# First preparation of a fused attention and expert kernel: remaining keys behind the first head, weight words behind the keys

## The chip, the cores and the metric

The kernel runs on one core of a Trainium2 chip. The metric is the device time of one execution in microseconds. Before the change three executions took 706.53, 705.54 and 706.43 us, a median of 706.43 us.

## The reference

Attention over 2 batches, 8 heads, 576 positions and a head size of 64, with a threshold: scores further than tau below a row's maximum are set aside before the softmax. Its output, 1152 tokens of 512, goes through a max of three linear layers and an output layer, and then through four experts of 1024 hidden units, weighted by normalised shares. All of it is asked for in float32; tau is 0.02, and the first layers' weights arrive as float64.

```python
scores = scale * q @ k.T
thresh = scores.max(-1, keepdims=True) - tau
scores = where(scores >= thresh, scores, -1e9)
attn = exp(scores - scores.max(-1, keepdims=True)); attn /= attn.sum(-1, keepdims=True) + 1e-9
x = (attn @ v).transpose(0, 2, 1, 3).reshape(1152, 512)
x = maximum(maximum(x @ w1, x @ w2), x @ w3) @ w_out
p = probs / (probs.sum(-1, keepdims=True) + 1e-9)
out = sum(p[:, e:e+1] * (maximum(x @ m_w1[e], 0) @ m_w2[e]) for e in range(4))
```

## The kernel before, in words

Every float32 product is made of three float32r products: each operand is cut into a high part (a rounded copy, made by ScalarE) and a low part (the rest, made by VectorE or GpSimd).

The program has three regions. **Region A** is the attention of batch 0 (`attention_fast`, L583): four jobs of two heads each, 9 steps to a job, 36 steps. A step makes one tile of scores, 128 query rows by 576 keys: `qk` (L382, four matmuls on TensorE), `peak` (L407, the row maximum, VectorE), `power` (L417, the exponential, ScalarE), `weigh` (L421, threshold and row sum, VectorE), `norm` (L427, GpSimd), `turn` (L437, transposes on TensorE), `cut_hi` and `cut_lo` (L477, L491), and per group of steps `gather` (L516, the product with the values). In this region the order of instructions on each engine is chosen by the framework's scheduler from a simulated timeline, except where `tc.issue_after(x)` puts an instruction behind x on x's engine. **Region B** holds the layers on batch 0's tokens and, woven in, the attention of batch 1; there the order on TensorE, VectorE, ScalarE and GpSimd is the order in the program. **Region C** is the rest of batch 1's tokens. The queue of SyncE (SP), which issues most DMAs, is ordered by the scheduler throughout.

Job 0 has a preparation of its own, `prep_first` (L283). `load_first` (L185) loads head 0's keys, the remaining 64 keys of both heads (`krem`, L193) and head 1's keys on SP, and the same of the queries (`qnat`, `qrem`) on ScalarE's queue. 512 of the 576 keys of a head are the main part. `head(h)` (L296) cuts a head's queries (`split`, L291: L292 copies keys, L293 the high part, L294 the low part), transposes keys (L300) and queries (L302), and writes the high keys (L305), the queries (L306) and the low keys (L307). The remaining keys go through L312 and L313 (transposes), L317 and L318. `qk` of step 0 needs all of head 0 and the remaining keys. Before any data is there, `spin` (L197) runs 14 matmuls on a constant tile; more follow behind the scores of steps 1, 2 and 3, 22, 8 and 8 of them (`SPINS_A`).

The layers' work follows a plan in columns of matmul work: `plan.at(when, fn)` files a function, and `stream.flush(when)` calls all that are due. A float64 weight block goes through the stages of `block` (L759): `words` (L775, load 512 KB as 32-bit words on SP), `exponent` (L791, ScalarE), `clamp` (L801, GpSimd), `low3` (L798), `merge` (L804) and `sign` (L809) on VectorE, `keep` (L813, stores the float32 block to DRAM for region C on SP: L818 for the first layers, L821 for the output layer), `hi` (L765, ScalarE) and `lo` (L769, GpSimd). The first three blocks are due before region A's steps: `stream.flush(-55000)` calls two `words`, `stream.flush(-READY)` the third and the stages of all three. `load_probs` and `norm_probs` (L1262, L1270) load and normalise the experts' shares. `sums_ahead` (L964) loads kept blocks on ScalarE's queue, adds quarters of them on GpSimd (L962) and stores the sums (L982).

Of the kernel before, what the change touches and what calls it, by code (L numbers as in the profile page):

```python
# [22 lines left out]
def fused_kernel(ctx: ExitStack, tc: tile.TileContext, q, k, v, tau, w1, w2, w3, w_out, probs, m_w1, m_w2, out):  # L23
# [46 lines left out]
    SPINS, SPINS_A = 14, (22, 8, 8)  # L70
# [114 lines left out]
    def load_first(job):  # L185

        for nm, src, eng in (("k", k, nc.sync), ("q", q, nc.scalar)):
            n = 2 if nm == "k" else 1
            t = atile([P, 2, NC, n, D], F32, "KN" if n == 2 else "qnat")
            r = atile([P, n, D], F32, f"{nm}rem")  # L190
            main = src[job.b, 2 * job.p:2 * job.p + 2, 0:MAIN, :].rearrange("h (p c) d -> p h c d", c=NC)
            eng.dma_start(out=t[:, 0, :, 0, :], in_=main[:, 0])
            eng.dma_start(out=r[:, 0, :], in_=src[job.b, 2 * job.p:2 * job.p + 2, MAIN:S, :])  # L193
            eng.dma_start(out=t[:, 1, :, 0, :], in_=main[:, 1])
            job.raw[nm] = (t, r)
# [86 lines left out]

    def prep_first(job):  # L283
# [12 lines left out]
        def head(h):  # L296
            split(QN[:, h * NC:(h + 1) * NC], qt[:, h, :, 0, :], kt[:, h])
            tk, tq = ptile_at("U", [P, MAIN]), ptile_at("U", [P, MAIN])
            for c in range(NC):
                nc.tensor.transpose(tk[:, c * P:(c + 1) * P], flat(kt[:, h, c]), ident)  # L300
            for c in range(NC):
                nc.tensor.transpose(tq[:, c * P:(c + 1) * P], flat(QN[:, h * NC + c]), ident)  # L302
            ko, qo = (0, W + REM)[h], (0, W + 2 * REM)[h]
            d1 = K1[:, ko:ko + MAIN]
            nc.scalar.activation(out=d1, in_=tk, func=AF.Copy)  # L305
            nc.scalar.activation(out=QS[:, qo:qo + MAIN], in_=tq, func=AF.Copy, scale=qscale)  # L306
            nc.vector.tensor_tensor(out=K2[:, ko:ko + MAIN], in0=tk, in1=f32(d1), op=ALU.subtract)  # L307

        head(0)
        split(QN[:, 2 * NC:], qr, kr[:, None])  # L310
# [6 lines left out]
        nc.scalar.activation(out=k1r, in_=trk, func=AF.Copy)  # L317
        nc.vector.tensor_tensor(out=k2r, in0=trk, in1=f32(k1r), op=ALU.subtract)  # L318
        yield
        head(1)  # L320
# [100 lines left out]
    def weigh(st):  # L421

        sv, _, ev = views(st)
        nc.vector.scalar_tensor_tensor(  # L424
            out=ev, in0=sv, scalar=st.stat["thr"], in1=ev, op0=ALU.is_ge, op1=ALU.mult, accum_out=st.stat["sum"])
# [157 lines left out]
    def attention_fast(jobs, modes):  # L583
# [5 lines left out]
        load_first(jobs[0])  # L589
        stream.flush(-55000)  # L590
        load_job(jobs[0], "v")
# [3 lines left out]
        for _ in start:  # L595
            pass
        stream.flush(-READY)
        back.add(values(jobs[0]))
# [10 lines left out]
        for i in range(n + 3):  # L609
# [34 lines left out]
            if nxt:  # L644
                at["raised"] = power(st)
                if i == n - NEARLY:
                    at["nearly"] = at["raised"]
# [5 lines left out]
            if nxt:  # L653
                weigh(st)
                if i:
                    turn(steps[i - 1])
            if st and not nxt:
# [101 lines left out]
    def block(use, shape, tag, bufs, load, lags, name=None, g=0, src=None, apart=False):  # L759
# [15 lines left out]
        def words():  # L775
            b["words"] = mo["words"].tile(shape + [2], U32, tag="words", name="words", bufs=NW)
            with ExitStack() as held:
                if "fourth" in at:
                    held.enter_context(tc.issue_after(at["fourth"].ins))
                nc.sync.dma_start(out=b["words"], in_=src)  # L780
# [32 lines left out]
        def keep():  # L813
# [5 lines left out]
            else:  # L819
                kept[name] = dp.tile(shape, F32, name=f"kept_{name}")  # L820
                nc.sync.dma_start(out=kept[name], in_=b["raw"])  # L821
# [262 lines left out]
    def max_mixed():  # L1084
# [31 lines left out]
        for f in range(0, NF, 2):  # L1116
            for w in range(3):
                ahead = f == 0 or w > 0
                for c in range(2 if ahead else 0):
                    sums_ahead(MAX0 + 6000 + AHEAD * k, (f"w{w}_{f // 2}", c), lambda w=w, f=f, c=c: kept[f"w{w}_{f // 2}"][:, c::2])  # L1120
# [3 lines left out]
        for f in range(0, NF2 // 2, 2):  # L1124
            for c in range(2):
                rows = m_w1[0].rearrange("(j c p) f -> c p j f", j=2, p=P)[c]
                sums_ahead(MAX0 + 6000 + AHEAD * k, (f"e{f}", c), lambda f=f, rows=rows: rows[:, :, f * P:(f + 2) * P].rearrange("p j (i f) -> p j i f", i=2))
# [164 lines left out]
    plan.at(MAX0 - 60000, norm_probs)  # L1292
# [101 lines left out]
```

## Time and profile before

| | |
|---|---|
| three executions | 706.53, 705.54, 706.43 us; median 706.43 |
| the profiled execution: its own time, its span | 707.25 us, 705.4 us |
| busy, share of the span | TensorE 98%, VectorE 67%, ScalarE 52%, GpSimd 70% |
| DMA | 95.17 MB, mean 135 GB/s |

The span runs from the first to the last instruction of the program; the execution's own time is 1.85 us longer. TensorE is busy in nearly all of it, so the places where it is idle, and the stretches in which it does work that serves nothing but its clock, are few and can be counted one by one. The page prints the granted clock in tenths of full speed.

### The profile page before, as it was taken

Reading aid. Unit: us, or ns where it says so; the run is one execution under the profiler, and the core shown is the slowest. Engines: PE = TensorE matmul, PEld = TensorE weight load, DVE = VectorE, ACT = ScalarE, POOL = GpSimd, SP = SyncE. Lnnn points to the kernel's source line nnn. Section 1 sums busy time; section 2 is a strip of 40 time slices with the busy share of each in tenths; the row PEclk is TensorE's granted clock in tenths of the full one; section 3 lists DMA queues with packets and bytes.
Section 4 is the critical chain, followed back from the end, with each engine's and each line's share of the span. In section 5 each row is a group of like instructions: output and inputs, shape, how many; then the busy total and the mean of one; then the engine's idle time right before and its main releaser. Section 6 shows DMA issues by size and latency. Waiting matters only on the chain.

```text
span 705.4 us, 11938 instructions
## 1 busy us (share of the span) xinstructions
PE 692.7 (98%) x3975; PEld 614.7 (87%) x3975; DVE 470.6 (67%) x1056; ACT 365.7 (52%) x774; POOL 493.4 (70%) x567
## 2 busy tenths in 40 slices
PE   7999999999999999999999999999999999999997
PEld 7988888877778888888888889999998998998996
DVE  5998898875467767677676567874644644653653
ACT  5989875544455555474545344446533433433430
POOL 4879876876585657576586477778569669669660
PEclk9999999999999999999999999999999999999999
DMA  6764506977888458365433643453122222322103
GB/s 185 181 140 97 150 1 201 276 228 224 229 225 218 118 140 231 109 174 152 120 120 89 213 158 123 150 165 122 58 90 90 77 74 90 91 66 88 56 1 75
DMA packets 108808, 95.17 MB, mean 135 GB/s; under 512 B 27340, under 2 KB 91852, under 8 KB 108748
## 3 DMA queue, kind: packets, MB, share of 16 engines
q1 hardware_dynamic: 91498, 83.24, 41.4%
q10 hardware_dynamic: 17218, 11.18, 5.4%
q8 instruction: 32, 0.52, 0.3%
q14 instruction: 28, 0.23, 0.1%
q0 software_dynamic: 32, 0.00, 0.0%
HBM read 69.09 MB, written 13.37 MB: 117 GB/s over the span
## 4 chain that ended last, share of the span: by engine, by line
PE 77%; POOL 7%; ACT 4%; DVE 4%; issue 4%; DMA 3%; SPq 0%; POOLq 0%; DVEq 0%; ACTq 0%
PE ps L1245 64%; PE u L534 5%; PE s L401 4%; PE t L441 3%; POOL a L769 3%; DMA raw<-in_moe_w_dram 1%; ACT em L419 1%; POOL hl L875 1%; POOL b L801 1%; DMA K<-KN 1%; ACT a L765 1%; POOL em L431 1%; DVE raw L809 1%; DMA krem<-in_k_dram 1%; DVE em L424 1%
## 5 line engine op out<-in xcount | busy, mean ns | idle before, releaser
L1245 PE MATMUL ps<-b,hh 128*128 128x512 f32 (+1 forms) x584 | 185.0, 391 | 0.0
L769 POOL TENSOR_TENSOR b<-raw,b 128x512 fp32r<-128x512 f32 x64 | 82.9, 1301 | 67.8 <-ACT b L765 67.7
L1245 PEld LDWEIGHTS ps<-b,hh 128*128 128x128 f32 x584 | 108.4, 188 | 20.8
L1245 PE MATMUL ps<-b,hl 128*128 128x512 f32 (+1 forms) x292 | 114.1, 391 | 0.0
L769 POOL TENSOR_TENSOR a<-raw,a 128x512 fp32r<-128x512 f32 (+1 forms) x58 | 72.8, 1257 | 35.8 <-ACT a L765 33.6
L1209 DVE SCALAR_TENSOR_TENSOR acc<-ps,pr,acc 128x512 f32<-128x512 f32 (+1 forms) x64 | 47.4, 741 | 73.2 <-PE ps L1245 72.9
L431 POOL TENSOR_SCALAR em<-em,st_r,one 128x576 f32<-128x576 f32 x70 | 58.0, 830 | 43.7 <-DVE st_r L430 35.7
L419 ACT ACTIVATE em<-s,st_negm 128x576 f32<-128x576 f32 x72 | 53.6, 744 | 60.4 <-DVE st_negm L412 53.1
L1245 PE MATMUL ps<-y0h,a 128*128 128x512 f32 x256 | 83.7, 400 | 0.3 <-POOL a L769 0.3
L412 DVE TENSOR_REDUCE st_negm<-s 128x1 f32<-128x576 f32 x72 | 54.2, 754 | 33.6 <-PE s L401 32.6
L1245 PE MATMUL ps<-bt,sh 128*128 128x320 f32 x300 | 69.9, 309 | 0.0
L424 DVE SCALAR_TENSOR_TENSOR em<-s,st_thr,em 128x576 f32<-128x576 f32 x72 | 58.6, 814 | 12.1 <-ACT em L419 10.8
L1030 POOL TENSOR_TENSOR sl<-s,sh 128x512 fp32r<-128x512 f32 x50 | 64.6, 1313 | 0.0
L1245 PEld LDWEIGHTS ps<-b,hl 128*128 128x128 f32 x292 | 54.9, 188 | 10.3
L765 ACT ACTIVATE a<-raw 128x512 fp32r<-128x512 f32 (+1 forms) x66 | 39.5, 603 | 36.7 <-DVE raw L809 14.2
L1017 POOL TENSOR_TENSOR dl<-wraw,dh 128x512 fp32r<-128x512 f32 (+1 forms) x50 | 50.1, 1023 | 8.3 <-ACT dh L1012 8.3
L1136 ACT ACTIVATE hh<-ps 128x320 fp32r<-128x320 f32 x64 | 27.4, 439 | 54.5 <-DVE ps L1063 54.5
L1245 PEld LDWEIGHTS ps<-y0h,a 128*128 128x128 f32 x256 | 47.2, 189 | 9.4 <-POOL a L769 0.8
L1245 PE MATMUL ps<-y0l,a 128*128 128x512 f32 x128 | 51.4, 401 | 0.0
L1245 PEld LDWEIGHTS ps<-bt,sh 128*128 128x128 f32 x300 | 51.1, 188 | 0.0
L401 PE MATMUL s<-K,QS 128*128 128x288 f32 x264 | 49.3, 309 | 1.4 <-DVE em L424 0.7
L1245 PE MATMUL ps<-x0h,a 128*128 128x512 f32 (+1 forms) x168 | 46.4, 363 | 0.7 <-POOL a L769 0.7
(227 smaller groups left out, 1723.5 us busy)
## 6 DMA issues: line engine op xcount, KB each, us to landing
raw<-in_moe_w_dram SPq DMA_DIRECT2D x96, 256.0 KB, 2.8
words<-in_moe_w_dram SPq DMA_DIRECT2D x18, 512.0 KB, 4.0
wraw<-in_moe_w_dram SPq DMA_DIRECT2D x16, 512.0 KB, 3.4
kept_w<-raw SPq DMA_DIRECT2D x18, 256.0 KB, 3.0
wraw<-kept_w SPq DMA_DIRECT2D x9, 512.0 KB, 3.6
K<-KN SPq DMA_DIRECT2D x14, 288.0 KB, 5.3
K<-KN SPq DMA_DIRECT2D x14, 256.0 KB, 4.1
sraw<-kept_w ACTq DMA_DIRECT2D x14, 256.0 KB, 3.9
```

Source lines behind the costliest of these rows:

```text
L401: st.whole = nc.tensor.matmul(st.s[:, kh, 0:HS], lhsT=l, rhs=r, start=i == 0, stop=i == len(terms) - 1)
L412: nc.vector.tensor_reduce(out=st.stat["negm"], in_=views(st)[0], op=ALU.max, axis=AX.XY, negate=True)
L419: return nc.scalar.activation(out=ev, in_=sv, func=AF.Exp, bias=st.stat["negm"])
L424: nc.vector.scalar_tensor_tensor(out=ev, in0=sv, scalar=st.stat["thr"], in1=ev, op0=ALU.is_ge, op1=ALU.mult, accum_out=st.stat["sum"])
L431: last = (nc.vector if swift else nc.gpsimd).tensor_scalar(out=em, in0=em, scalar1=re, scalar2=one, op0=ALU.mult, op1=ALU.mult)
L534: at["valued"] = nc.tensor.matmul(pv, lhsT=l, rhs=r, start=i == 0, stop=i == len(terms) - 1)
L765: nc.scalar.activation(out=b["hi"], in_=b["raw"], func=AF.Copy)
L769: nc.gpsimd.tensor_tensor(out=b["lo"], in0=b["raw"], in1=f32(b["hi"]), op=ALU.subtract)
L1017: nc.gpsimd.tensor_tensor(out=rows(b["dl"], x), in0=src, in1=f32(rows(b["dh"], x)), op=ALU.subtract)
L1030: nc.gpsimd.tensor_tensor(out=rows(b["sl"], slice(x, x + 2)), in0=rows(b["s"], slice(x, x + 2)), in1=f32(rows(b["sh"], slice(x, x + 2))), ...
L1209: nc.vector.scalar_tensor_tensor(out=accs[t][:, cols], in0=ps, scalar=pe, in1=accs[t][:, cols], op0=ALU.mult, op1=ALU.add)
L1245: nc.tensor.matmul(banks[x], lhsT=l, rhs=r, start=i == 0, stop=i == count - 1)
```

## The change

- `load_first` remembers the loads of the remaining keys and queries. The first `words` load gets a dependency on both: it is issued when they have landed.
- The values of job 0 are loaded ahead of the `words`.
- The split of the remaining queries and keys is issued behind head 0's last instructions on ScalarE and VectorE (`behind`). Head 1's query transposes, copies and low keys are issued behind the remaining keys' copies and behind step 0's scores.
- The third `words`, the stages of the three blocks and the values' cut are called after step 0's `weigh` and issued behind step 0's `power` on ScalarE and `weigh` on VectorE.
- The spins behind step 1's scores go from 22 to 14.
- `norm_probs` goes from 60000 columns ahead of `MAX0` to 24000 behind it (`MAX0` is where the plan's output layer ends).
- The output layer's kept blocks are stored from ScalarE's queue and no longer from SP.
- `sums_ahead` goes 22000 columns later.

```diff
-    SPINS, SPINS_A = 14, (22, 8, 8)
+    SPINS, SPINS_A = 14, (14, 8, 8)
...
-            eng.dma_start(out=r[:, 0, :], in_=src[job.b, 2 * job.p:2 * job.p + 2, MAIN:S, :])
+            at["rest", nm] = eng.dma_start(out=r[:, 0, :], in_=src[job.b, 2 * job.p:2 * job.p + 2, MAIN:S, :])
...
+    def behind(*steps):
+        held = ExitStack()
+        for x in steps:
+            held.enter_context(tc.issue_after(x.ins))
+        return held
...
-        def head(h):
+        def head(h, *held):
             split(QN[:, h * NC:(h + 1) * NC], qt[:, h, :, 0, :], kt[:, h])
...
-            nc.vector.tensor_tensor(out=K2[:, ko:ko + MAIN], in0=tk, in1=f32(d1), op=ALU.subtract)
-
-        head(0)
-        split(QN[:, 2 * NC:], qr, kr[:, None])
+            with behind(*held):
+                for c in range(NC):
+                    nc.tensor.transpose(tq[:, c * P:(c + 1) * P], flat(QN[:, h * NC + c]), ident)
+                nc.scalar.activation(out=d1, in_=tk, func=AF.Copy)
+                stacked = nc.scalar.activation(out=QS[:, qo:qo + MAIN], in_=tq, func=AF.Copy, scale=qscale)
+                return stacked, nc.vector.tensor_tensor(out=K2[:, ko:ko + MAIN], in0=tk, in1=f32(d1), op=ALU.subtract)
+
+        with behind(*head(0)):
+            split(QN[:, 2 * NC:], qr, kr[:, None])
...
-        nc.scalar.activation(out=k1r, in_=trk, func=AF.Copy)
-        nc.vector.tensor_tensor(out=k2r, in0=trk, in1=f32(k1r), op=ALU.subtract)
+        high = nc.scalar.activation(out=k1r, in_=trk, func=AF.Copy)
+        low = nc.vector.tensor_tensor(out=k2r, in0=trk, in1=f32(k1r), op=ALU.subtract)
         yield
-        head(1)
+        head(1, high, low, (yield))
...
+        load_job(jobs[0], "v")
         stream.flush(-55000)
-        load_job(jobs[0], "v")
         start = prep_first(jobs[0])
         next(start)
         qk(steps[0])
-        for _ in start:
+        next(start)
+        try:
+            start.send(steps[0].whole)
+        except StopIteration:
             pass
-        stream.flush(-READY)
-        back.add(values(jobs[0]))
...
-                weigh(st)
+                weighed = weigh(st)
                 if i:
                     turn(steps[i - 1])
+                else:
+                    with behind(raised, weighed):
+                        stream.flush(-READY)
+                        back.add(values(jobs[0]))
+                        back.advance(2)
...
-                nc.sync.dma_start(out=b["words"], in_=src)
+                load = nc.sync.dma_start(out=b["words"], in_=src)
+            for nm in "" if kept.setdefault("words", 0) else "kq":
+                tc.add_manual_dep(load.ins, at["rest", nm].ins.name, ...)
+            kept["words"] = 1
...
-                nc.sync.dma_start(out=kept[name], in_=b["raw"])
+                nc.scalar.dma_start(out=kept[name], in_=b["raw"])
...
-                    sums_ahead(MAX0 + 6000 + AHEAD * k, ...
+                    sums_ahead(MAX0 + 28000 + AHEAD * k, ...
...
-    plan.at(MAX0 - 60000, norm_probs)
+    plan.at(MAX0 + 24000, norm_probs)
```

## Rows read from the trace of the kernel before

**Rows 1.** Waits of TensorE over the span: us in total, times, longest us.
```profile
PE t L312 <- DVE krem L292: 2.4, 1, 2.4
PE ps L1245 <- POOL a L769: 1.5, 3, 0.7
```

**Rows 2.** The chain that ended last, from 0 to 60 us: start, us, what.
```profile
1.51 5.91 DMA krem<-in_k_dram
...
7.44 0.21 DVE krem L292
...
7.69 0.48 PE t L312
```

**Rows 3.** Busy us in stretches: PE, PEld, DVE, ACT, POOL; granted clock, DMA share, GB/s.
```profile
5.00:10.00 5.00, 2.57 (x13) 2.04 (x11) 2.61 (x9) 1.87 (x6) 0.00 (x0) 1.00 0.98 314
...
20.00:25.00 5.00, 4.99 (x40) 4.40 (x39) 4.97 (x16) 4.60 (x12) 3.31 (x4) 1.00 0.80 173
...
200.00:700.00 500.00, 500.00 (x2830) 448.63 (x2830) 316.31 (x677) 231.95 (x495) 345.03 (x372) 1.00 0.41 120
```

**Rows 4.** Instructions in order of time, 0 to 32 us: start, us, engine, line.
```profile
2.83 2.38 SPq L780 DMA_DIRECT2D words<-in_moe_w_dram  x2
...
4.06 0.42 ACT L293 ACTIVATE em<-qnat 128x256 fp32r<-128x256 f32 x1
...
4.21 1.05 PE L300 MATMUL u<-ident,KN 128*128 128x128 f32 x4
...
5.26 0.86 SPq L163 DMA_DIRECT2D vnat<-in_v_dram  x1
...
7.55 0.42 DVE L294 TENSOR_TENSOR em<-qnat,em 128x256 f32<-128x256 f32 x1
...
8.02 1.11 PE L302 MATMUL u<-ident,em 128*128 128x128 f32 x4
...
9.16 0.69 DVE L798 TENSOR_SCALAR t<-words 128x512 uint32<-128x512 uint32 x1
9.17 0.69 ACT L306 ACTIVATE QS<-u,qscale 128x512 fp32r<-128x512 f32 x1 [1.51 <-PE u L302]
...
10.06 0.29 DVE L318 TENSOR_TENSOR K<-t,K 128x128 fp32r<-128x128 f32 x1 [0.22 <-ACT K L317]
...
11.27 0.83 PE L401 MATMUL s<-K,QS 128*128 128x288 f32 x2
...
11.72 0.68 DVE L798 TENSOR_SCALAR t<-words 128x512 uint32<-128x512 uint32 x1
...
11.78 1.27 SPq L167 DMA_DIRECT2D knat<-in_k_dram  x2
...
13.66 2.70 PE L199 MATMUL u<-still 128*128 128x224 f32 x22
...
17.64 0.60 PE L213 MATMUL u<-ident,knat 128*128 128x128 f32 x4
```

**Rows 5.** Instructions in order of time, 146 to 178 us.
```profile
146.50 0.18 DVE L1272 TENSOR_REDUCE tot<-pr 128x9 f32<-128x36 f32 x1
...
148.68 0.68 DVE L867 TENSOR_TENSOR hmax<-ps,hmax 128x512 f32<-128x512 f32 x1
...
153.19 0.73 PE L1245 MATMUL ps<-x0h,a 128*128 128x512 f32 x2 [0.70 <-POOL a L769]
```

**Rows 6.** Instructions in order of time, 178 to 203 us.
```profile
192.86 0.57 ACTq L982 DMA_DIRECT2D kept_sw<-hmax  x1
...
194.90 0.66 PE L441 MATMUL t<-ident,em 128*128 128x128 f32 x4 [0.55 <-POOL em L431]
```

**Rows 7.** The matmuls of L199: count, shortest, median, longest ns, first and last start.
```profile
L199 PE MATMUL u<-still x38: 263/274/353, 13.7 to 20.4; 128*128 128x224 f32 x38
L199 PE MATMUL s<-still x14: 415/415/555, 1.1 to 4.0; 128*128 128x224 f32 x14
```

**Rows 8.** Loads by line over the span: count, KB each, median us to landing.
```profile
knat<-in_k_dram SPq DMA_DIRECT2D x14, 128.0 KB, 3.0
```

More of the change, by code (lines that the diff above doesn't have):

```diff
@@ L300, in head @@
                 nc.tensor.transpose(tk[:, c * P:(c + 1) * P], flat(kt[:, h, c]), ident)
-            for c in range(NC):
-                nc.tensor.transpose(tq[:, c * P:(c + 1) * P], flat(QN[:, h * NC + c]), ident)
             ko, qo = (0, W + REM)[h], (0, W + 2 * REM)[h]
             d1 = K1[:, ko:ko + MAIN]
-            nc.scalar.activation(out=d1, in_=tk, func=AF.Copy)
-            nc.scalar.activation(out=QS[:, qo:qo + MAIN], in_=tq, func=AF.Copy, scale=qscale)
-            nc.vector.tensor_tensor(out=K2[:, ko:ko + MAIN], in0=tk, in1=f32(d1), op=ALU.subtract)
-        head(0)
-        split(QN[:, 2 * NC:], qr, kr[:, None])
+            with behind(*held):
[6 more added lines that the diff above has]
+            split(QN[:, 2 * NC:], qr, kr[:, None])
         tr = ptile_at("T", [P, 2, P])
@@ L423, in weigh @@
         sv, _, ev = views(st)
-        nc.vector.scalar_tensor_tensor(
+        return nc.vector.scalar_tensor_tensor(
             out=ev, in0=sv, scalar=st.stat["thr"], in1=ev, op0=ALU.is_ge, op1=ALU.mult, accum_out=st.stat["sum"])
@@ L644, in attention_fast @@
             if nxt:
-                at["raised"] = power(st)
+                at["raised"] = raised = power(st)
                 if i == n - NEARLY:
@@ L779, in words @@
                     held.enter_context(tc.issue_after(at["fourth"].ins))
-                nc.sync.dma_start(out=b["words"], in_=src)
+                load = nc.sync.dma_start(out=b["words"], in_=src)
+            for nm in "" if kept.setdefault("words", 0) else "kq":
+                tc.add_manual_dep(
+                    load.ins, at["rest", nm].ins.name, mybir.DependencyInfo(mybir.DependencyClass.Sync, mybir.DependencyReason.DATA),
+                    reason="first keys and queries")
+            kept["words"] = 1
             ix = (slice(None),) * len(shape)
@@ L1119, in max_mixed @@
                 for c in range(2 if ahead else 0):
-                    sums_ahead(MAX0 + 6000 + AHEAD * k, (f"w{w}_{f // 2}", c), lambda w=w, f=f, c=c: kept[f"w{w}_{f // 2}"][:, c::2])
+                    sums_ahead(MAX0 + 28000 + AHEAD * k, (f"w{w}_{f // 2}", c), lambda w=w, f=f, c=c: kept[f"w{w}_{f // 2}"][:, c::2])
                     k += 1
@@ L1126, in max_mixed @@
                 rows = m_w1[0].rearrange("(j c p) f -> c p j f", j=2, p=P)[c]
-                sums_ahead(MAX0 + 6000 + AHEAD * k, (f"e{f}", c), lambda f=f, rows=rows: rows[:, :, f * P:(f + 2) * P].rearrange("p j (i f) -> p j i f", i=2))
+                sums_ahead(MAX0 + 28000 + AHEAD * k, (f"e{f}", c), lambda f=f, rows=rows: rows[:, :, f * P:(f + 2) * P].rearrange("p j (i f) -> p j i f", i=2))
                 k += 1
```

## Prediction

> **What bounds the kernel now.** The page's busy shares come first: TensorE is busy for 98% of the span, about 693 of 705.4 us. So the list of its waits says what there is to win, and the longest is one wait of 2.4 us in the first preparation, in front of the transpose of the remaining keys [rows 1]. The chain of waits shows the same place from the other side: the load of those keys takes 5.91 us from issue to landing (1.51 to 7.42), then come a VectorE copy of 0.21 us and the transpose [rows 2]. The stretches show how the shortage moves: from 5 to 10 us no engine is busy for more than 2.6 of 5 us while the DMA engines are at 0.98; from 20 to 25 us TensorE (4.99) and VectorE (4.97) are both full; from 200 to 700 us TensorE is busy for 500.00 of 500 [rows 3]. Whatever the start wins can reach the end if region A lets it through, because what follows waits for TensorE alone. The other waits worth a change are three of 1.5 us together for weight blocks (L769) [rows 1], between 150 and 180 us.
>
> **The start, step by step.** Head 0's queries don't need the remaining keys, but their low part (L294) ran at 7.55, behind the copy of the remaining keys on VectorE, though its high part was done at 4.06 + 0.42 = 4.48 [rows 2, 4]. With the new order L294 runs at 4.5 to 4.9. The key transposes L300 end at 5.26, the query transposes L302 take 1.11 (to 6.4), the query copy L306 takes 0.69 (to 7.1) [rows 4]. Behind it come the remaining keys. I let them land at 7.42 as before: the copy of 0.21, the transpose of 0.48 [rows 2], the high copy, for which I take the 0.29 of L318, and L318 itself, 0.29, then the second half of step 0's scores, 0.83 [rows 4]: 2.1 us, so step 0's scores are done at 9.5. Before, they were done at 11.27 + 0.83 = 12.1 [rows 4]. That is 2.6 us earlier, and 3.0 if the keys land before the query copy is done.
>
> The hold on `words` frees the DMA engines, which were full, for the keys; it also takes from VectorE what filled its wait. Two of the nine word operations on VectorE, both of L798, began ahead of step 0's maximum, at 9.16 and 11.72, and took 0.69 and 0.68 [rows 4]: 1.4 us which now fall into the stretch where VectorE is full. So by VectorE's account the start wins 2.6 - 1.4 = 1.2 us. By TensorE's account no word operation counts, and it wins the wait of 2.4 us [rows 1] and eight spins: 22 took 2.70, so eight take 1.0 [rows 4]. That is 3.4. Both engines are full at 20 us [rows 3], and I take the nearer to VectorE, whose work is the one that the steps wait for first: 1.9 us, with 0 and 3.4 as the ends. Step 0 itself gains more than that, and its successors less. The values' cut, now behind step 0's `weigh`, has GpSimd's idle first 10 us to lose and nothing else: it is needed only at the first `gather`, after step 4.
>
> **The layers at 146 to 178 us.** `norm_probs` is four VectorE instructions of about 0.2 us each, the first at 146.50, and the next maximum of the layers (L867) starts at 148.68 with ScalarE's and GpSimd's part of the hidden rows behind it; GpSimd's block for the next product comes after that, and TensorE waits 0.70 for it at 153.19 [rows 5]. Taking 0.8 off VectorE moves that chain by between 0 and 0.7. I take 0.5, since the instruction that the chain runs through comes after two word operations that remain. At its new place, behind 24000 columns of the experts, VectorE has room (316 of 500 us) [rows 3]; without it the first totals would come 0.8 later, which nothing waits for at once.
>
> **The kept blocks' stores.** Eight issues leave SP for ScalarE. A store issue on ScalarE's queue takes 0.57 [rows 6], 4.6 us in all. Each stands behind `hi` of the same block, which waits for the same data, so it brings no wait of its own. ScalarE is 52% busy over the span, so I cost it at nothing. Without that cover a late `hi` could repeat a wait of 0.7 [rows 1] at most, and earlier loads on SP could win one; I keep -0.5 to +0.5.
>
> **The sums ahead.** Four GpSimd additions, a load and a store per half block leave the stretch from 184 us, where TensorE waits 0.55 for a GpSimd normalisation at 194.90 [rows 6]. They come back one by one later, where TensorE never waits [rows 3]. Between 0 and 0.55, and below nothing by as much if a later place turns into a wait: I take 0.3.
>
> **Sum.** 1.9 + 0.5 + 0 + 0.3 = 2.7 us. The profiled execution took 707.25 (its span 705.4 and 1.85 around it) and would take 704.55. It was 0.82 slower than the median of the executions, 706.43, and I forecast the median: 703.7.
>
> **Rivals.** [...]
>
> *VectorE, ScalarE and GpSimd absorb it.* The word operations meet an already full stretch, the scheduler orders region A anew, and the 36 steps end almost when they did. The start wins nothing, and what is left is some of the 0.8 of the later edits: 705.9. For it speaks the stretch at 20 us [rows 3]; against it, that region A starts earlier and its work does not grow.
>
> *Job 1's keys come late (slower).* The first `words` can't be issued before the remaining keys land, at 7.42 and not 2.83, and all behind them on SP waits too. The distance from the first `words` to job 1's keys is 11.78 - 2.83 = 8.95, less 0.86 for the values, which now go ahead [rows 4]: 15.5. Two issues take 1.27, and a landing takes 3.0 [rows 8]: 19.8. TensorE came to their transposes (L213) at 17.64 [rows 4] and would come at 15.7. If the scheduler leaves them there, TensorE stands for 4.1 us with all later steps behind it: 706.43 - 2.7 + 4.1 = 707.8. It decides once the keys land more than 2.7 us after TensorE gets to L213. Against it speak that the keys may land sooner without the `words` beside them, and that these transposes have more than ten microseconds until job 1's first scores. [...] This rival and my 7.42 go by the same landing.
>
> **How the numbers follow.** Forecast 0.55, clock 0.17, absorbed 0.19, late keys 0.09. The forecast's own range is 702.3 to 705.0. For 8 in 10 I go from 701.4, below the clock's case, to 706.4, which takes in the absorbed case and leaves the late keys out. A measurement of this kernel can tell about 0.2% (1.4 us) from no change. Faster than 705.0: the clock's case, nearly all of the forecast's and a little of the others, 0.70. Within 0.2%: most of the absorbed case and half of the late keys, 0.22. Slower than 707.8: 0.08.
>
> **What would show it.** L294 near 4.5 us and no wait of TensorE for L292 show the first step right; step 0's scores done by about 9.5 show the second. [...] The first matmul of region B's layers and the last of region A's steps some 2 us earlier show that region A lets the gain through; the same times as before show it absorbed. A wait at L213 for knat shows the late keys. The waits at 153 and 195 us should be gone. The prediction is wrong if region A's end does not move, or if the layers' waits for L769 grow past 1.5 us.

## The result, and the profile after

The changed kernel takes 715.27 us, the median of six executions (712.96 to 716.76), where the kernel before took 706.04 beside it (six executions, 705.32 to 707.40): a ratio of 1.0122, 95% interval 1.0108 to 1.0137. It is slower by some 9.2 us, and the prediction of 703.7 was wrong in sign. The profiled execution of after was the quickest of its six, 712.96 us with a span of 711.2, so its trace shows 5.7 us of loss against the profiled execution of before (707.25), and not the whole 9.2.

TensorE's longest waits over the span (us in total, times, longest) answer to [rows 1]:

```profile
PE u L306 <- DVE K L314: 1.8, 1, 1.8
PE ps L1263 <- POOL a L782: 1.3, 2, 0.8
PE t L448 <- DVE st_r L437: 1.2, 1, 1.2
```

The wait of 2.4 us for the remaining keys is gone. In its place stands one of 1.8 us, also in the first preparation, for head 0's low keys. The instructions of the start in order of time, which answer to [rows 4], show why:

```profile
5.15 0.42 DVE L300 TENSOR_TENSOR em<-qnat,em 128x256 f32<-128x256 f32 x1
5.62 0.87 PE L311 MATMUL u<-ident,em 128*128 128x128 f32 x4 [0.35 <-DVE em L300]
6.76 0.93 SPq L793 DMA_DIRECT2D words<-in_moe_w_dram  x2
6.98 0.42 ACT L299 ACTIVATE em<-qnat 128x256 fp32r<-128x256 f32 x1 [1.08 <-DMA qnat<-in_q_dram]
7.30 0.67 ACT L313 ACTIVATE QS<-u,qscale 128x512 fp32r<-128x512 f32 x1
7.34 0.29 DVE L298 COPY KN<-KN 128x256 f32<-128x256 f32 x1 [1.77 <-DMA KN<-in_k_dram]
7.55 0.68 DVE L314 TENSOR_TENSOR K<-u,K 128x512 fp32r<-128x512 f32 x1
8.15 0.18 DVE L298 COPY krem<-krem 128x64 f32<-128x64 f32 x1
...
8.29 0.66 PE L306 MATMUL u<-ident,KN 128*128 128x128 f32 x4 [1.80 <-DVE K L314]
...
9.80 0.93 PE L408 MATMUL s<-K,QS 128*128 128x288 f32 x2 [0.37 <-ACT K L324]
...
10.33 1.30 SPq L167 DMA_DIRECT2D knat<-in_k_dram  x2
...
12.37 1.33 PE L408 MATMUL s<-K,QS 128*128 128x288 f32 x4 [0.78 <-ACT QS L313]
13.50 3.08 PE L199 MATMUL u<-still 128*128 128x224 f32 x14
...
15.14 1.28 DVE L816 TENSOR_SCALAR t<-words 128x512 uint32<-128x512 uint32 x2
...
17.84 0.60 PE L213 MATMUL u<-ident,knat 128*128 128x128 f32 x4
...
23.36 0.63 PE L448 MATMUL t<-ident,em 128*128 128x128 f32 x4 [1.16 <-DVE st_r L437]
```

The remaining keys no longer hold head 0 up, but head 1 does. (TensorE's L306 at 8.29 is head 1's key transposes; the program writes them into the buffer that L314 reads, and they waited 1.80 us for L314.) On VectorE the copy of head 1's keys (L298 at 7.34, after 1.77 us of waiting for their load) stands ahead of head 0's low keys (L314), and on ScalarE head 1's high queries (L299 at 6.98) stand ahead of head 0's query copy (L313). Step 0's scores end at 9.80 + 0.93 = 10.73 us; before it was 12.1 [rows 4]. Of this lead of 1.4 us nothing is left at 23 us: the first transpose of weights (L448) comes at 23.36, and in before at 20.52 (L441).

Busy time by stretch (TensorE, its weight loads, VectorE, ScalarE, GpSimd, then the granted clock), of before and then of after; three stretches of after (from 5, from 20 and from 200 us) answer to [rows 3]:

```profile
10.00:15.00 5.00, 4.57 (x25) 4.20 (x25) 4.06 (x8) 4.86 (x12) 3.56 (x7) 1.00 0.74 191
15.00:20.00 5.00, 4.92 (x42) 4.64 (x41) 5.00 (x14) 2.81 (x5) 4.07 (x5) 1.00 0.54 147
```

```profile
5.00:10.00 5.00, 2.48 (x15) 1.72 (x13) 2.23 (x9) 2.26 (x6) 0.15 (x1) 0.95 0.68 215
10.00:15.00 5.00, 4.22 (x18) 3.78 (x19) 2.91 (x6) 3.84 (x9) 1.74 (x5) 0.50 1.09 253
15.00:20.00 5.00, 4.75 (x34) 4.51 (x34) 4.46 (x13) 2.95 (x6) 3.02 (x5) 0.87 0.19 53
20.00:25.00 5.00, 3.69 (x28) 2.96 (x27) 5.00 (x14) 3.49 (x9) 3.67 (x4) 1.00 0.84 221
...
200.00:700.00 500.00, 499.48 (x2825) 447.78 (x2824) 318.44 (x685) 233.72 (x501) 350.80 (x383) 1.00 0.42 121
```

Two things are new between 10 and 20 us. VectorE works for 2.91 and 4.46 us and not for 4.06 and 5.00, since the word operations begin at 15.14 and not at 9.16 [rows 4]; from 20 us on it is full, and TensorE waits. And the granted clock reads 0.50 from 10 to 15 us: its records show 1.00, here called the high level, from 6.10 to 9.51 us, and 0.50, the low one, from there to 16.34. The scores of step 1 took 1.33 us at the low level, those of step 2 0.70 at the high one. (Ahead of the first record of the clock its column reads 1.00. In before the first record, one of 1.00, begins at 13.84. That the clock was low ahead of it is inferred: step 1's scores, L401 at 12.53, took 1.33 us there too, and the matmuls of L199 were longer [rows 7].)

The rest of the loss is far from the start. The first transposes of weights are 2.8 us late and the last row maximum of region A 3.6 (L419 at 99.67, L412 in before at 96.11); from the sixth on, the row maxima between them are 1.7 to 4.9 us late, without steady growth. Behind the last maximum the delay nearly doubles. The next fences show TensorE from the start of region A's last maximum to the matmul behind its last `gather`: first before (96.11 to 105.87 us), then after (99.67 to 112.14), the costliest lines with their counts, and the busy times.

```profile
L534 PE MATMUL u<-am,V 128*128 128x320 f32 (+1 forms) x28 | 5.1, 305 | 0.3 <-POOL am L502 0.2
L441 PE MATMUL t<-ident,em 128*128 128x128 f32 x16 | 2.4, 276 | 0.0
...
96.11:105.87 9.76, 9.43 (x73) 8.74 (x71) 8.57 (x23) 6.67 (x18) 6.03 (x8) 1.00 0.01 3
```

```profile
L541 PE MATMUL u<-am,V 128*128 128x256 f32 (+1 forms) x36 | 6.2, 298 | 0.2 <-ACT am L494 0.2
L448 PE MATMUL t<-ident,em 128*128 128x128 f32 x20 | 2.9, 274 | 0.5 <-ACT am L513 0.5
...
99.67:112.14 12.47, 11.30 (x86) 10.29 (x85) 9.51 (x23) 9.43 (x23) 7.79 (x10) 1.00 0.01 2
```

After has nine products with the values (45 for 36, the line of the remaining keys' values, not shown, taken in) and four transposes (20 for 16) more to do behind its last maximum, and TensorE is idle there for 1.17 us and not 0.33. The work of region A is the same; its order isn't. The scheduler, which chooses the order of region A, laid all of it out anew: without the spins, the lists of TensorE's matmuls in before and after differ in places up to the 644th, close to the end of region A (its last `gather` is the 649th), and are the same behind it.

### The profile page after: what moved, and what is told of

It reads as the page before. It is cut to its first block, busy times and chain, and to the rows that moved or that the text cites. A ratio compares the mean times of both kernels' runs of the same rounds, so it can differ in the third digit from the quotient of the medians.

```text
span 711.2 us, 11916 instructions
## 1 busy us (share of the span) xinstructions
PE 693.5 (98%) x3967; PEld 614.3 (86%) x3967; DVE 471.9 (66%) x1056; ACT 366.0 (51%) x774; POOL 492.4 (69%) x567
## 4 chain that ended last, share of the span: by engine, by line
PE 76%; DVE 6%; POOL 6%; issue 5%; ACT 4%; DMA 1%; SPq 0%; DVEq 0%; POOLq 0%; ACTq 0%
PE ps L1263 63%; PE s L408 4%; PE u L541 4%; PE t L448 3%; POOL a L782 2%; DVE st_negm L419 1%; DVE em L431 1%; ACT a L778 1%; POOL hl L893 1%; ACT em L426 1%; POOL b L819 1%; DVE raw L827 1%; DVE bits L822 1%; DMA KN<-in_k_dram 1%; DMA raw<-in_moe_w_dram 1%
## 5 line engine op out<-in xcount | busy, mean ns | idle before, releaser
L419 DVE TENSOR_REDUCE st_negm<-s 128x1 f32<-128x576 f32 x72 | 54.3, 754 | 36.3 <-PE s L408 35.4
L431 DVE SCALAR_TENSOR_TENSOR em<-s,st_thr,em 128x576 f32<-128x576 f32 x72 | 58.5, 813 | 12.3 <-ACT em L426 10.4
L408 PE MATMUL s<-K,QS 128*128 128x288 f32 x264 | 49.1, 308 | 2.1 <-ACT QS L313 0.8
L408 PEld LDWEIGHTS s<-K,QS 128*128 128x128 f32 x264 | 40.8, 191 | 7.8 <-DVE em L431 1.5
```

Source lines behind the costliest of these rows:

```text
L408: st.whole = nc.tensor.matmul(st.s[:, kh, 0:HS], lhsT=l, rhs=r, start=i == 0, stop=i == len(terms) - 1)
L419: nc.vector.tensor_reduce(out=st.stat["negm"], in_=views(st)[0], op=ALU.max, axis=AX.XY, negate=True)
L431: return nc.vector.scalar_tensor_tensor(out=ev, in0=sv, scalar=st.stat["thr"], in1=ev, op0=ALU.is_ge, op1=ALU.mult, accum_out=st.stat["sum"])
```

## The experiments

Each ran beside the kernel before on the same chip. The table sets them by one property that can be read from the program: from which of TensorE's matmuls on (spins left out) the order is that of the kernel before. The tail is the time from the start of region A's last maximum to that of its last `gather` matmul; in the expectations it is counted to an earlier one (the 152nd of 160), where it reads 8 and 11. "Low until" is the time at which the high clock level came to stay in the profiled execution.

| kernel | order as before from | tail, us | clock low until | ratio to before, 95% interval |
|---|---|---|---|---|
| before | | 9.6 | 13.8 | 1 |
| late_only | 1st | 9.9 | 10.2 | 0.9999 (0.9986 to 1.0012) |
| before_spins14 | 1st | 9.6 | 12.0 | 0.9992 (0.9983 to 1.0000) |
| late_14 | 1st | 9.6 | 9.5 | 0.9999 (0.9987 to 1.0011) |
| early_28 | 59th | 9.9 | 15.6 | 1.0060 (1.0047 to 1.0073) |
| words_early | 121st | 9.8 | 18.2 | 1.0037 (1.0021 to 1.0053) |
| words_early_h1_gap | 121st | 9.6 | 19.1 | 1.0038 (1.0026 to 1.0050) |
| early_gap8 | 139th | 9.9 | 18.7 | 1.0032 (1.0021 to 1.0043) |
| before_20_spins | 216th | 9.8 | 16.0 | 1.0020 (1.0011 to 1.0028) |
| spins22 | 216th | 9.9 | 16.9 | 1.0051 (1.0031 to 1.0070) |
| spins22_gap | 613th | 11.3 | 5.1 | 1.0049 (1.0035 to 1.0064) |
| words_early_gap | 645th | 11.6 | 18.6 | 1.0038 (1.0025 to 1.0052) |
| early_h1_gap_22 | 645th | 11.6 | 18.2 | 1.0066 (1.0054 to 1.0079) |
| before_12_spins | 645th | 12.3 | 11.0 | 1.0056 (1.0043 to 1.0070) |
| before_16_spins | 645th | 12.3 | 11.2 | 1.0054 (1.0040 to 1.0067) |
| after_gap | 645th | 12.3 | 6.5 | 1.0074 (1.0056 to 1.0092) |
| after_h1 | 645th | 12.3 | 14.7 | 1.0091 (1.0067 to 1.0114) |
| no_hold | 645th | 12.3 | 18.0 | 1.0119 (1.0094 to 1.0145) |
| after | 645th | 12.3 | 16.3 | 1.0122 (1.0108 to 1.0137) |
| low3_sbuf | 645th | 12.3 | 18.2 | 1.0140 (1.0117 to 1.0163) |

### The later edits alone, the words alone, the tiles, the spins

**late_only** is the kernel before with the three edits outside the start.

```diff
-                nc.sync.dma_start(out=kept[name], in_=b["raw"])
+                nc.scalar.dma_start(out=kept[name], in_=b["raw"])
...
-    plan.at(MAX0 - 60000, norm_probs)
+    plan.at(MAX0 + 24000, norm_probs)
```

> The kernel before with the three later edits alone (shares normalised 84000 columns later, the output layer's kept blocks stored from ScalarE's queue, the sums ahead 22000 columns later). If the loss comes from the start, as I hold: 705 to 706.5 us, that is 0 to 1 us faster than before, by the gain of 0.6 us that the trace of after shows between its 112 us (+6.3) and its end (+5.7). If the later edits carry the loss: 712 or more.

It took 705.76 us against 706.46: no difference that can be told. By this run the whole loss comes from the start's edits.

**words_early** puts the words' stages and the values' cut of the changed kernel back ahead of step 0.

```diff
+        stream.flush(-READY)
+        back.add(values(jobs[0]))
...
-                else:
-                    with behind(raised, weighed):
-                        stream.flush(-READY)
-                        back.add(values(jobs[0]))
-                        back.advance(2)
```

> The changed kernel with one part undone: the third words load, the stages of the first three blocks and the values' cut are called right after the first preparation, as before, and not behind step 0's weigh. Theory 'banks and debt' (word operations behind step 0 leave VectorE idle from 10 to 15 us, and then hold both T banks of PSUM until 23.2 us, so that the first turn waits): most of the loss goes, 706 to 709 us, and the first turn comes at 21 us or earlier. Theory 'clock' (the low level from 9.5 to 16.3 us is the loss): still 713 or more, since TensorE's idle time ahead of 10 us stays. Theory 'order' (any new order of region A costs): 711 to 716, first turn early but region A long.

It took 708.99 us, 2.5 above before, so it takes back some 6 us of 9. Taken alone that looks like the price of VectorE's late word operations. The table says more: region A also came back to the order of before, and from its 20th `gather` matmul on every one stands 2.6 to 3.0 us behind before's.

**low3_sbuf** lets the three early blocks work in their own tile, so that they take no PSUM bank from the transposes.

```diff
-            pool, tag = (at["T"], "T") if kept["blocks"] <= EARLY else (mo["bits"], "bits")
-            b["low3"] = pool.tile([P, 512], U32, tag=tag, name=tag.lower())...
+            if kept["blocks"] <= EARLY:
+                b["low3"] = b["low"]
...
```

> The changed kernel with the first three blocks' shifted words written in place into the words tile and not into a T bank of PSUM, so that no turn waits for a bank. Theory 'banks': the first turn comes at 18 to 20 us and not 23.4, and the time is 709 to 712 us. Theory 'debt' without the banks (VectorE is behind by 2 us at 25 us): first turn earlier, time 713 to 715. Theory 'clock': 714 to 716.

It took 716.66 us, no faster than after, so nothing speaks for the banks as the price. It doesn't refute them cleanly: this kernel drew an order of its own, which differs from that of after in places up to the 386th matmul. Its first transposes come 0.9 us earlier than in after (22.42), its last maximum 3.7 us later (103.33).

**spins22** is the changed kernel with 22 spins again behind step 1's scores.

```diff
-    SPINS, SPINS_A = 14, (14, 8, 8)
+    SPINS, SPINS_A = 14, (22, 8, 8)
```

> The changed kernel with 22 spins behind step 1's scores, as before. Theory 'clock': if the spins at the low level (14 took 3.08 us) are what keeps step 2 back, 8 more at 0.21 us each make it 1.7 us slower, 716 to 718 us; if they are what brings the high level back, it comes no later than 16.3 us and the time is 714 to 716. Theory 'banks and debt': 714 to 717, the first turn at 23 us or later all the same.

It took 710.11 us, so eight more spins made it 5 us faster. The gain isn't at the start: its first transposes come at 24.02 (after: 23.36) and its last maximum at 99.62 (after: 99.67). It lies behind that maximum, in a tail of 9.9 and not 12.3 us, in the order of before. The tail accounts for 2.5 of the 5.2 us between the medians; the two profiled executions (711.47, the slowest of its four, and after's quickest) are 1.5 apart, so no trace shows the rest.

### The hold, the clock, head 1

**no_hold** issues the first words at once. The order on TensorE and VectorE stays that of after.

```diff
-            for nm in "" if kept.setdefault("words", 0) else "kq":
+            for nm in "":
```

> The changed kernel without the hold of the first words load on the landing of the remaining keys and queries: the load is issued as soon as SP comes to it, and the order of instructions on TensorE and VectorE stays that of the changed kernel. Theory debt (the word operations are placed behind step 0's weigh, whatever the data do): the same as the changed kernel, 715 (713 to 717), first L816 near 15.1, first turn near 23.4. Rival hold (the words' data come late and make VectorE idle from 10 to 15 us): first L816 near 12 to 13, first turn 1.5 to 2.5 us sooner, 711 to 713. Rival traffic (the hold is what brings the remaining keys in time): remaining keys land 0.5 to 1 us later, step 0's scores end near 11.5, 716.

715.2 us: the hold costs nothing and wins nothing that these four executions (713.41 to 717.45) can tell. The first L816 came at 15.58. The copy of the remaining keys came at 7.71 (after: 8.15), with no wait of VectorE for their load in either kernel, and that of head 1's keys, which wait for theirs in both, at 6.90 (after: 7.34). So the first words, issued at 4.08 and in after at 6.76, made neither copy late in this execution.

**after_gap** puts ten spins behind head 0's query transposes, into the stretch where TensorE waited for L314.

```diff
+        first = head(0)
+        with behind(at["turned0"]):
+            spin(at["spun"], 10)
-        with behind(*head(0)):
+        with behind(*first):
```

> The changed kernel with ten more spins on the constant tile, placed behind head 0's query transposes, so that TensorE has work from 6.5 to 8.3 us, where it waited for head 1. Theory clock (the granted clock falls back to 0.5 at 9.5 because TensorE had stood before, and the low level from 9.5 to 16.3 makes scores and transposes of steps 0 to 2 late): the clock stays at 1.0 from 6 us on or rises once and stays, step 1's scores take 0.9 and not 1.33, first turn 1.5 to 2.5 us sooner, 711 to 713. Theory debt (VectorE's order sets the steps, the clock doesn't matter): the clock may change, but the first turn stays within 0.5 of 23.4 and the time at 715 (713.5 to 716.5).

711.90 us, 3.4 less than after. The records now show the high level from 6.53 to 709.67 us, and step 1's scores take 0.80 and not 1.33 us. TensorE and VectorE from 10 to 20 us:

```profile
10.00:15.00 5.00, 4.10 (x31) 3.70 (x31) 4.11 (x8) 4.44 (x10) 2.32 (x4) 1.00 1.13 263
15.00:20.00 5.00, 4.04 (x32) 3.58 (x32) 5.00 (x15) 3.00 (x7) 3.58 (x7) 1.00 0.39 91
```

VectorE has back the 1.2 us that it lacked from 10 to 15 us, and the first transposes come at 21.45, 1.9 earlier than in after. The first `gather` matmul is even 0.8 us ahead of before's. Yet the last one is 5.4 us late, so with the clock high more than half of the loss is still there. It isn't the tail alone: from 20 to 25 us VectorE is full (5.00) as in after and TensorE does 3.41 of 5 us, and by the 20th `gather` the delay is 4.9. Nor is the clock the only difference from after, since this kernel's order differs from it in places up to the 386th matmul.

**after_h1** issues head 1's split behind head 0's copies.

```diff
-        def head(h, *held):
-            split(QN[:, h * NC:(h + 1) * NC], qt[:, h, :, 0, :], kt[:, h])
+        def head(h, *held, first=()):
+            with behind(*first):
+                split(QN[:, h * NC:(h + 1) * NC], qt[:, h, :, 0, :], kt[:, h])
...
-        head(1, high, low, (yield))
+        head(1, high, low, (yield), first=first)
```

> The changed kernel with head 1's split (L298 to L300) issued behind head 0's copies, so that no instruction which waits for head 1's data stands ahead of head 0's copies on ScalarE and VectorE. Theory head of line (step 0's scores were 1.2 us later than predicted because L313 and L314 stood behind head 1's copies): step 0's scores end near 9.7 and not 10.73. What it brings to the end: by theory debt 0 to 0.5 us (VectorE waits for the word operations anyway), 714.5 to 715.5; by the prediction's own working 1.2 us, 714; if the scheduler orders region A's tail anew, some 3 us more, as with 22 spins.

The low keys and step 0's scores in this kernel:

```profile
6.12 0.69 DVE L315 TENSOR_TENSOR K<-u,K 128x512 fp32r<-128x512 f32 x1
...
9.10 0.93 PE L410 MATMUL s<-K,QS 128*128 128x288 f32 x2 [0.37 <-ACT K L326]
```

L315 runs at 6.12 and not at 7.55, and the scores end at 10.03. So head 1's data did stand in the way. The time is 713.1 us; its interval just meets that of after, so 2 us are likely and not shown. The order, too, differs from that of after in places up to the 215th matmul.

**words_early_h1_gap** joins the edits of words_early and after_h1 with six spins in the gap.

```diff
+            spin(at["spun"], 6)
...
+        stream.flush(-READY)
+        back.add(values(jobs[0]))
...
-        head(1, high, low, (yield))
+        head(1, high, low, (yield), first=first)
```

> All three causes taken away together: the changed kernel with words and values placed as before the change (ahead of step 0), head 1's split behind head 0's copies, and six more spins behind head 0's query transposes. The kernel with the words alone back at their place took 708.99. If the debt, the fall of the clock and the head of line are the whole loss and add up: clock high from about 6 us or at the latest from 13, step 0's scores by 9.7 to 10.5, first turn at 19 to 20.5, and 703 to 706. If the clock doesn't matter for the steps: first turn near 21.5 to 22, 708. If region A's tail is drawn anew by the scheduler and is long (11 us from the last maximum to the last gather and not 8): 3 us on top of either.

708.61 us: no better than words_early alone. The clock fell back all the same, from 12.24 to 19.07 us, so this run doesn't tell how much the clock is worth.

### The clock with the order of before

Four kernels were to separate the clock from the order. **spins22_gap** and **words_early_gap** add the ten spins of after_gap to spins22 and words_early; **before_spins14** takes only the change's edit of the spins; **early_h1_gap_22** joins words_early, head 1 behind head 0's copies, ten spins in the gap and 22 behind step 1, as a candidate to beat both kernels. The lines of before_spins14, and those that the other three share:

```diff
-    SPINS, SPINS_A = 14, (22, 8, 8)
+    SPINS, SPINS_A = 14, (14, 8, 8)
```

```diff
+        with behind(at["turned0"]):
+            spin(at["spun"], 10)
```

> The changed kernel with 22 spins in front of job 1's preparation as before the change and ten more behind head 0's query transposes. With 22 spins alone it took 710.11, its region A came in the order of the kernel before (110 gather matmuls ahead of the 36th step's scores, where the changed kernel has 100), all of it 3.5 us late, and the clock was low from 10.1 to 16.9 us. The words still stand behind step 0's weigh. Theory clock: with the clock at 1.0 throughout, the start loses 2.5 to 3.5 us less, 706.5 to 707.5. Theory debt (the words behind weigh cost the 3.5 us whatever the clock is): 709 to 710, gathers 3 to 3.5 us later than before.

> The changed kernel with words and values at their place before the change, and ten more spins behind head 0's query transposes. Without these spins it took 708.99, region A in the order before, 2.7 us late, the clock low from 8.0 to 18.2 us and TensorE busy for 5.00 of 5 us from 15 to 20. Theory clock: with the clock at 1.0 from about 6 us on, the 2.7 us go, 705.5 to 706.8. Theory first preparation (the new order of the heads itself costs the 2.7 us): 708.5 to 709.5. If the clock falls back again at 12 to 13, as with six spins: 708 to 709, and nothing is told.

> The kernel before with 14 and not 22 spins in front of job 1's preparation; nothing else. Theory clock by the spins (these eight spins are what brings and keeps the high level): the clock rises at 16 to 20 us and not at 13.8, region A 2 to 3 us late in the same order, 708.5 to 709.5. Rival (the rise and fall of the clock come from the first preparation's new order, the eight spins don't matter): high from 10 to 14 us, 705.5 to 706.5.

> A candidate to beat both: the changed kernel with words and values at their place before the change, head 1's split behind head 0's copies, ten more spins behind head 0's query transposes and 22 spins in front of job 1's preparation. It keeps of the change the new order of the first preparation and the three later edits. If clock, words and head of line are the whole loss: step 0's scores by 9.8, clock at 1.0 from about 6 us on, first turn at 19 to 20, region A in the order before, 704.5 to 706. If the new order of the first preparation costs by itself: 707.5 to 709.

They took 709.94, 709.09, 706.09 and 710.94 us. Three fall into a range given ahead: spins22_gap into that of the late words (709 to 710), words_early_gap into that of the first preparation (708.5 to 709.5) and before_spins14 into its rival's. But only before_spins14 came out the way its theory had it, with eight spins fewer costing nothing; the two others had drawn orders that no theory held, and early_h1_gap_22 missed both its ranges. In spins22_gap the granted clock was 1.00 from 5.1 us on and the first `gather` 0.6 us ahead of before, yet region A ended 2.6 us late. The three kernels with spins in the gap had drawn new orders, and their tails are 11.3 to 11.6 us. The theory that the clock is most of the loss fell here, and the order became the one to test.

### The order alone

Two spins more or fewer at the very start of the *unchanged* kernel suffice to give region A the order of after, from the 360th matmul to its end; six more leave it in that of before from the 216th on. These kernels have nothing of the change in them.

```diff
-    SPINS, SPINS_A = 14, (22, 8, 8)
+    SPINS, SPINS_A = 16, (22, 8, 8)
```

(12 and 20 in the two others.)

> The kernel before with 16 and not 14 spins at the very start; nothing of the change is in it. With these two spins the order of TensorE's matmuls (spins left out) comes out as the changed kernel's from its 360th on, with 100 and not 110 gather matmuls ahead of the 36th step's scores. Theory order (the new order of region A costs some 3 us by itself, in its tail): the last maximum near 96, the last gather 11 us behind it and not 8, 709 to 710. Rival (order is harmless; the 3 us come with the change's own edits): 706 to 707.

> The kernel before with 12 and not 14 spins at the very start, nothing of the change in it. The order of TensorE's matmuls is the changed kernel's from the 360th on (100 gather matmuls ahead of the 36th step's scores), as with 16 spins. Theory order: 709.5 to 711, tail from the last maximum to the last gather 11 us. Rival (more spins at the start, not the order, cost the 4 us of 16 spins): 706 or less.

> The kernel before with 20 and not 14 spins at the very start, nothing of the change in it. The order of TensorE's matmuls is that of the kernel before from the 216th on (110 gather matmuls ahead of the 36th step's scores). Theory order: 706 to 707.5, tail 8 us; up to 1 us of it for head 0's transposes behind six more spins. Rival (more spins at the start cost, not the order): 711 or more.

They took 710.40 us with 16 spins, 709.88 with 12, and 707.35 with 20. Both kernels with the order of after lose 3.8 to 4.0 us; the one with the most spins and the order of before loses 1.3. So it isn't the spins. The tail of 16 spins (97.36 to 109.83 us) has the rows of after to the count:

```profile
L534 PE MATMUL u<-am,V 128*128 128x256 f32 (+1 forms) x36 | 6.2, 299 | 0.2 <-ACT am L487 0.2
L441 PE MATMUL t<-ident,em 128*128 128x128 f32 x20 | 2.9, 274 | 0.5 <-ACT am L506 0.5
...
97.36:109.83 12.47, 11.29 (x85) 10.28 (x84) 9.50 (x23) 9.42 (x23) 7.79 (x10) 1.00 0.00 1
```

Its first transposes come at 20.63 us, as in before (20.52), its last maximum 1.3 us late and its last `gather` 4.0 us late. This is the order's price with the start left as it was. From 20 us to the end of the tail TensorE is idle for 5.8 us and not for 2.9 as in before; the other 1 us of the 4 is longer busy time, for no more matmuls (612 recorded, in before 617). The order was compared on TensorE alone, and that of the other engines may differ with it.

**early_gap8** (words_early with eight spins in the gap) and **early_28** (words_early with 28 spins at the very start) keep the order of before. Beside the edit of words_early, the first has that of after_gap with the count below, the second the other line.

```diff
+            spin(at["spun"], 8)
```

```diff
-    SPINS, SPINS_A = 14, (14, 8, 8)
+    SPINS, SPINS_A = 28, (14, 8, 8)
```

> The changed kernel with words and values at their place before the change and eight more spins behind head 0's query transposes; the order of TensorE's matmuls is that of the kernel before from the 139th on. With none it took 708.99, with ten 709.09, there with region A in another order. Theory clock: if it is high from 12 us or earlier to stay, region A starts within 0.5 us of before, 705.5 to 707. If it falls back until 18, as with none and with ten: 708 to 709.

> The changed kernel with words and values at their place before the change and 28 and not 14 spins at the very start, so that TensorE works from 1.1 us until head 0 is prepared; the order of its matmuls is that of the kernel before from the 59th on. Theory clock: the high level is reached before 8 us; if it stays, the start is 0.7 us or more ahead of before, 704.5 to 706. Theory first preparation (its new order loses by itself, with clock and order as before): 707.5 to 709.

709.01 and 710.92 us. In early_gap8 the clock fell back at 11.86 until 18.69. In early_28 the long row of spins delayed head 0's key transposes to 6.34, and TensorE then waited 4.46 us for L313; it says nothing of the first preparation as such. From 15 to 20 us TensorE is full in words_early (first fence) and in early_gap8 (second), at a mean granted clock of 0.68 and 0.63:

```profile
15.00:20.00 5.00, 5.00 (x32) 5.00 (x31) 4.20 (x12) 2.37 (x6) 3.12 (x5) 0.68 0.61 149
```

```profile
15.00:20.00 5.00, 5.00 (x30) 5.00 (x30) 4.59 (x10) 3.01 (x7) 3.36 (x5) 0.63 0.51 131
```

In before it did 42 matmuls in these 5 us, here 32 and 30. That fits a start that is late because TensorE is slow there. A kernel with the new first preparation, the order of before and the high level throughout wasn't obtained in a profile, so the two aren't cleanly parted. The ten executions of words_early give an estimate: the three with a mean granted clock of 1.000, so with next to no return to the low level, took 707.58 to 708.02 us, and the seven with 0.992 to 0.999 took 708.52 to 711.86. By that some 1.2 us over before's 706.46 stay without the return, and about 2 come with it (medians 707.66 and 709.60). When the clock first rose in them isn't on record.

**late_14** joins the two edits that lost nothing, on the kernel before: those of late_only and

```diff
-    SPINS, SPINS_A = 14, (22, 8, 8)
+    SPINS, SPINS_A = 14, (14, 8, 8)
```

> The kernel before with the three later edits of the change (norm_probs, kept blocks' stores, sums ahead) and with 14 and not 22 spins in front of job 1's preparation; the order of TensorE's matmuls is that of the kernel before throughout. The two alone gave 705.76 against 706.46 and 706.09 against 706.68. If both are gains: 705.3 to 705.8, a ratio of 0.998 to 0.999. If both were the moment at which the clock rose: 706 to 706.7, a ratio of 1.

706.26 against 706.39 us. No kernel of the study is clearly faster than the kernel before.

## Why the prediction was wrong

**The step that failed** is the sum for the start, "1.9 us, with 0 and 3.4 as the ends". A new order of region A stands only in the rival of the absorbed gain, where it takes back the gain and no more; against it stood "region A starts earlier and its work does not grow". So the sum had no loss in it for the order. The runs put that loss at 3.8 to 4.0 us with no change of the work (16 and 12 spins). In the changed kernel 715.27 against 710.11 with spins22 suggests 5 us, of which the traces show 1.5 to 2.5. By the runs on the unchanged kernel it is the largest term of the 9.2 us.

**The first preparation** lost instead of winning. With the words at their old place and the order of before, it stands 2.2 to 2.6 us behind before in three kernels (words_early, words_early_h1_gap, early_gap8). In the profiled execution of all three the clock was low until 18 to 19 us. How much is the clock and how much the new order of the heads stays open; the executions of words_early suggest a good 1 us for the heads and the rest for the clock.

**Step 0's scores** were to be done at 9.5 and were done at 10.73. The low queries ran at 5.15, not 4.5 to 4.9, behind a wait of 1.02 us for tau; the remaining keys' wait did go. That wait was itself not the same in every execution: late_14, which has the order of before on every engine up to there, shows 0.84 us of it and not 2.4. What failed is the list of what is late next: head 1's loads, which the change leaves ahead of head 0's last copies in both engines' order. after_h1 brings 0.7 us of it back.

**VectorE's 1.4 us of word operations** were seen, and their place too, but not that VectorE would stand idle first: it lacks 1.15 us of work from 10 to 15 us (2.91 against 4.06), and TensorE pays from 20 us on (3.69 busy of 5; before 4.99 [rows 3]). The words' new place is worth about 1 us by spins22 against words_early (710.11 and 708.99); that isn't shown, as their intervals overlap and they differ in spins and order too. The eight spins, 1.0 us in TensorE's account, brought nothing clear (before_spins14: 706.09 against 706.68, the interval up to 1.0000).

**The clock's case**, which got a chance of 0.17, was a high level that comes sooner and makes the start faster. The level did come early, at 6.10 us. It went low again at 9.51, which no case held; between the two, TensorE's longest idle time was the 1.80 us in front of L306. Its chance and the low end for 8 in 10, 701.4, count on a gain by an early high level, and no run shows one: spins22_gap, with a granted clock of 1.00 from 5.1 us on, took 709.94 us, and after_gap, high from 6.53 on, 711.90. That the start is slower when the level goes low again is likely (after_gap's first transposes come 1.9 us earlier than after's), not shown.

**The rival of the absorbed gain** named the place, the scheduler's new order, but gave it no price beyond the gain: 705.9. **Late keys of job 1** did not come: with the hold, their load was issued at 10.33 us, and L213 ran at 17.84 without a wait; before, these were 11.78 and 17.64 [rows 4].

**The later edits** were put at 0.8 us and brought nothing that can be told (late_only, late_14). TensorE's waits for weight blocks are 1.3 us in two pieces where they were 1.5 in three [rows 1]; the wait at 195 us [rows 6] is gone in after, but late_14 still has one of 0.9 us for GpSimd in that stretch. The stores at nothing were right as far as these runs can tell.

**What adds up.** The order 4 to 5, the first preparation with its clock 2.2 to 2.6, the words about 1: 7.2 to 8.6 of 9.2 us. This takes the parts to add, which no run shows; with 5 for the order they are the steps from after over spins22 and words_early to before, and add up by the way they were formed. Only the 4 from the unchanged kernel stands apart from that. The rest is within the spread of the executions of after, nearly 4 us, and isn't settled.

## What to carry to other kernels

Where a scheduler lays out a long region from a simulated timeline, an edit at its head has two prices: its own, and that of the order that it happens to draw. Draw the order again with an edit that changes no work (two spins more or fewer) before crediting or blaming the change; here that alone was worth 4 us, more than all the gains that were forecast together (2.7). And when an instruction that waits is moved out of the way of those behind it, look at which load the next instruction waits for: here VectorE then waited 1.77 us for head 1's keys, ahead of head 0's low keys.

## What the runs showed of the hardware

TensorE's high clock level (a granted clock of 1.00) did not stay in all of these kernels, once reached; the low one is 0.50. In after the high level lasted from 6.10 to 9.51 us and came back at 16.34; in words_early_h1_gap from 5.42 to 12.24 and again at 19.07; in before_spins14 from 5.12 to 8.54 and again at 11.95. With ten spins behind head 0's query transposes, where TensorE waited 1.80 us in after, it stayed in after_gap (high from 6.53 on); with the same ten it did not in words_early_gap (low from 11.78 to 18.61). These are the times of one execution each: late_only and before run the same program there, and the rise came at 10.15 and 13.84. The six executions of after have mean granted clocks from 0.992 to 1.000 with no order in their times (714.08 and 715.05 us at 0.992, 715.50 at 1.000), so the return alone doesn't explain their spread. Step 1's scores took 1.33 us at the low level (after, L408 at 12.37) and 0.80 at the high one (after_gap, at 11.63).
